# Loads of one quad put behind the inverse sums of two others, one product moved to VectorE, and the order of TensorE's products drawn anew

## Chip, cores and metric

One core of a Trainium2 chip runs the whole kernel as one program. The metric is the time of one execution on the device in microseconds, the median of several runs. The kernel takes the inputs of the reference and gives its output in float32.

## What is computed

An attention with normalised queries and keys, and behind it a pair of matrix products with h·cos(h) between them:

```python
q, k, v: (8, 12, 448, 64) float32;  tau = 0.1
q_n = q / (norm(q, axis=-1) + 1e-6);  k_n = k / (norm(k, axis=-1) + 1e-6)
scores = matmul(q_n, k_n.T) / tau
attn = exp(scores - max(scores)); attn = attn / (sum(attn) + 1e-9)
x = matmul(attn, v) with heads joined: (3584, 768)
h = x @ w_in                # (3584, 2048)
out = (h * cos(h)) @ w_out  # (3584, 768)
```

## The kernel before

**Stages.** The work goes by the 8 batches, c = 0 to 7. `m1` makes x @ w_in of a batch: 8 pairs of blocks of 128 columns, each block 6 products of TensorE (96 in all), and behind each pair ScalarE and VectorE make h·cos(h) into the tile gT (L701 and L705 on ScalarE, L703 and L707 on VectorE). `m2` makes the product with w_out: half-outputs of 16 products of 384 columns each (six or eight to a batch, by turns), each ended by a copy of PSUM into osb on VectorE (L725) and a store.

**Attention by quads.** Four heads form a quad; there are 24, three to a batch, so batch 2 needs quads 6, 7 and 8. A quad goes through these steps. `load_qk` (L402) brings Q and K through SP's DMA queue into one of three buffers each. `norm_a` squares them on GpSimd (L450) and sums the squares on VectorE (L454). `norm_b` makes the inverse norms (ScalarE L472 and L484, VectorE L487 and L490) and scales Q and K on GpSimd (L511). `turn` transposes both by DMA on SP's queue (L550). `scores` is a group of 4 products of TensorE that run side by side (L568), one group for each of the 7 parts of a quad, each followed by one exponential of 896 columns on ScalarE (L575). `av` multiplies all 7 parts with V (28 products, L585), and VectorE copies the result into AVs (L594), of which there are four.

**Inverse sums.** For quads 6 to 23 two quads share a round, as quads 8 and 9 do. `sums` makes the sums of the exponentials with 28 products (L646); `invert` takes logarithm and exponential on ScalarE (L659, L661) into the one tile Zs, spreads Zs with four DMAs to a quad into R (L667, two buffers, one for even and one for odd quads), and multiplies AVs with R into xT on GpSimd (L670). `m1` of a batch reads xT. For its first pair (or the first two) the products with the first two quads of the batch go ahead (`EARLY`), those with the third quad follow.

**The order on TensorE** is the order of the program text. While `m2` of batch c runs, the table `VISITS[c]` says how the quads of the next batches are let in: an entry (n, more) takes n items from the stream of quads, then `more` products of `m2`. `LATER` says at which part of the next quad a quad's `av` stands. The first part of a quad calls `begin`, which issues the steps that prepare the later quads: `norm_b` and `turn` of the quad two ahead, `load_qk` of the quad four ahead, `norm_a` of the quad three ahead. Score groups and `av` share three pairs of PSUM banks in turn: an item waits until the one that used its pair three items earlier has been read, by ScalarE or, for an `av`, by VectorE.

**The order on the other engines and on SP's and GpSimd's DMA queues** is made by the class `Planner` when the program is built: each operation carries a reckoned duration, each DMA a reckoned transfer time (`moves`) besides a first and a last part of 1.2 and 0.8, and the planner plays the program through and lets each engine take what is ready and due soonest. That order is then fixed; each engine waits at each instruction for what it needs. Operations with `lock=True` are not planned beside one another on VectorE and GpSimd. `lead` makes an operation due earlier.

Of the kernel before, what the change touches and what calls it, by code (L numbers as in the profile page):

```python
# [8 lines left out]
ACT = mybir.ActivationFunctionType  # L9
# [12 lines left out]
class Planner:  # L22
# [21 lines left out]
    def op(self, eng, dur, fn, r=(), w=(), after=(), dma=None, moves=0, mode="f", chain=None, keep=False, lead=0.0,  # L44
           packet=74, lock=False, key=None):
        if key is None:
            self.count += 1
            key = self.count - 1
            if self.strict:
                key += self.MOVE.get(key, 0)  # L50
            if self.count - 1 in self.FILL:
                self.idle(*self.FILL[self.count - 1], key - 0.01)
        o = Op()
        o.i, o.eng, o.dur, o.fn, o.dma, o.moves, o.mode, o.chain = (
            len(self.ops), eng, dur, fn, dma, moves, mode, chain)
        o.lat = self.FIRST + moves + self.LAST if dma else self.LAT[eng]
        o.behind, o.lead, o.packet, o.lock = None, lead, packet, lock
        o.key = key
        if keep or self.strict and eng in ("act", "dve", "pool", "sp"):
            self.tail.setdefault(eng, []).append(o)  # L60
        o.reads, o.writes = tuple(r), tuple(w)
        deps = {a.i for a in after if a is not None}
        for x in o.reads:
            if x in self.last_write:
                deps.add(self.last_write[x].i)
        for x in o.writes:
            if x in self.last_write:
                deps.add(self.last_write[x].i)
            deps.update(p.i for p in self.readers.get(x, ()))
        deps.discard(o.i)  # L70
        o.deps = sorted(deps)
        for x in o.reads:
            self.readers.setdefault(x, []).append(o)
        for x in o.writes:
            self.last_write[x] = o
            self.readers[x] = []
        self.ops.append(o)
        return o
# [200 lines left out]
def bass_cosine_attention__then__act_gcu_kernel(  # L279
# [31 lines left out]
    def ring(name, n, shape, dt):  # L311
        return [sb("%s%d" % (name, i), shape, dt) for i in range(n)]
# [20 lines left out]
    Zs = ring("Zs", 1, [128, S], F32)  # L333
    R = ring("R", 2, [128, 2, S], F32)
# [15 lines left out]
    op = P.op  # L350
# [19 lines left out]
    def table(m):  # L370
        if mode[0] == m:
            return
        mode[0] = m
        op("act", 1.3, lambda e: e.add_instruction(mybir.InstLoadActFuncSet(
            name=nc.get_next_instruction_name(), act_func_set_id={"exp": 6, "sin": 9}[m], engine=e.engine)),
           w=["table"])

    def act(m, dur, fn, r=(), w=(), **kw):
        table(m)
        return op("act", dur, fn, r=[*r, "table"], w=w, **kw)  # L380
# [16 lines left out]
    def load_one(qd, w, part=ALL[0], after=()):  # L397
        b, h0, s = qd // QB, 2 * (qd % QB), qd % 3
        src, dst, nm = ((q, Qf, "Qf"), (k, Kf, "Kf"))[w]
        j0, j1 = part  # L400
        ap = bass.AP(src.tensor, (b * NH + h0) * S * D + j0 * D, [[NJ * D, 128], [NH // 2 * S * D, 2], [1, (j1 - j0) * D]])
        return op("sp", 0.6, lambda e: e.dma_start(dst[s].ap()[:, :, j0:j1].rearrange("p r j d -> p r (j d)"), ap),  # L402
                  w=cut(nm, s, part), dma=(nm, s, j0), moves=0.17 * (j1 - j0), after=after)

    def load_qk(qd, after=()):
        return [load_one(qd, w, after=after) for w in range(2)]
# [30 lines left out]
    def square(qd, w, eng, part=ALL[0], after=()):  # L437
        s, u = qd % 3, qd % 2
        j0, j1 = part
        n = (j1 - j0) / NJ  # L440
        f, sq, nm = ((Qf, sqq, "Q"), (Kf, sqk, "K"))[w]
        src = f[s].ap()[:, :, j0:j1]
        dst = sq.ap().rearrange("p (r j) d -> p r j d", r=2)[:, :, j0:j1]
        if part == ALL[0]:
            src, dst = src.rearrange("p r j d -> p (r j) d"), sq.ap()
        if eng == "act":
            op("act", 0.1 + 0.83 * n, lambda e: e.activation(dst, src, ACT.Square), r=cut(nm + "f", s, part),
               w=cut("sq" + nm, 0, part))
        else:
            op(eng, (1.68 if eng == "pool" else 1.05) * n, lambda e: e.tensor_tensor(dst, src, src, ALU.mult),  # L450
               r=cut(nm + "f", s, part), w=cut("sq" + nm, 0, part), after=after, lock=True)

        def add():
            return op("dve", 0.07 + 0.95 * n, lambda e: e.tensor_reduce(  # L454
                out=n2.ap()[:, u, H * w:H * w + H] if part == ALL[0] else jr(n2, u, w, part),
                in_=dst, axis=AX.X, op=ALU.add),
                r=cut("sq" + nm, 0, part), w=cut("n2%d" % w, u, part))

        return add
# [55 lines left out]
    def norm_a(qd):  # L515
        for w in range(2):
            square(qd, w, "pool")()
# [28 lines left out]
    def turn(qd, after=()):  # L546

        u = qd % 3
        for n, t, nm in ((Qn, qT, "Q"), (Kn, kT, "K")):
            op("sp", 1.3, lambda e, n=n, t=t: e.dma_start_transpose(  # L550
                t[u].ap().rearrange("p j a x -> p j (a x)"), n[0].ap().rearrange("p j r d -> p (j r d)")),
               r=cut(nm + "n", 0, ALL[0]), w=cut(nm + "T", u, ALL[0]), dma=(nm + "T", u), moves=1.1, packet=18,
               after=after)
# [42 lines left out]
    Z, LEAD = 6, 15.0  # L596
# [58 lines left out]
    def invert(quads, bk):  # L655
        z = 0
        np_ = 2 * len(quads)
        zz = Zs[z].ap()[0:32 * np_, :]
        act("exp", 0.44, lambda e: e.activation(zz, bank(bk, S, 0, 32 * np_), ACT.Ln, bias=0.0, scale=1.0),  # L659
            r=whole(bk), w=[("Zs", z)], lead=LEAD)  # L660
        act("exp", 0.47, lambda e: e.activation(zz, zz, ACT.Exp, bias=0.0, scale=-1.0), r=[("Zs", z)], w=[("Zs", z)], lead=LEAD)  # L661
        for i, qd in enumerate(quads):
            u, sl, b = qd % 2, qd % NA, qd // QB
            for r in range(2):
                for a in range(2):
                    src = bass.AP(Zs[z], (64 * i + 32 * r + 16 * a) * S, [[S, 16], [0, 4], [1, S]])
                    op("sp", 0.6, lambda e, r=r, a=a, u=u, src=src: e.dma_start(R[u].ap()[64 * r:64 * r + 64, a, :], src),  # L667
                       r=[("Zs", z)], w=[("R", u, r, a)], dma=("R", u, r, a), moves=0.5, packet=140, lead=LEAD)
            c0 = 2 * (qd % QB)
            op("pool", 2.04, lambda e, u=u, sl=sl, b=b, c0=c0: e.tensor_tensor(  # L670
                xT[b % 2].ap()[:, c0:c0 + 2, :], AVs[sl].ap(), R[u].ap(), ALU.mult),
                r=[("AV", sl), *(("R", u, r, a) for r in range(2) for a in range(2))], w=[("x", b % 2, qd % QB)], lead=LEAD, lock=True)

    def round_(quads, bk):
        sums(quads, bk)
        invert(quads, bk)

    INV2PI = 1.0 / (2.0 * math.pi)
    GUARD = 1.0 - 4e-6
# [52 lines left out]
    def store(t, x0, x1, parts, engs=("sp", "sp")):  # L732
        so = t % 3
        for sg, eng in enumerate(engs):
# [8 lines left out]
    ROUNDS = [[i, i + 1] for i in range(6, NQ, 2)]  # L743
    VISITS = [
# [7 lines left out]
        [],  # L752
        [],
    ]
    LATER = {19: 3, 18: -1, 5: 3, 7: -1, 21: -2, 9: 4, 10: -2, 12: -2, 22: -1, 23: 4, 15: -2, 13: 3, 16: 1, 17: 4, 8: 1}
    E1, E2 = NNB - 6, NNB - 4
    due = []
    cur = [7]
# [1 line left out]
    def now():  # L760
        return [[o for o in P.ops if o.eng == "pe"][-1]]

    def begin(qd):
        if qd + 2 < NQ:
            norm_b(qd + 2)
            turn(qd + 2)
        if qd < NQ - 4:
            load_qk(qd + 4)
        if qd + 3 < NQ:
            norm_a(qd + 3)  # L770

    AFTER, SLOTS = 2, 3
    stream = []
# [3 lines left out]
    def quad_slots(qd):  # L777
        slots = [("s", NJ * qd + j) for j in range(NJ)]
        if qd > FIRST and qd - 1 not in closed:
            n = AFTER + LATER.get(qd, 0)  # L780
            slots[n:n] = [("z", qd - 1)] * (qd - 1 in DIRECT) + [("v", qd - 1)]
# [53 lines left out]
    gate = load_qk(1)  # L835
# [139 lines left out]
    done = FIRST  # L975
    for c in range(B):
# [59 lines left out]
        done = new  # L1036
# [46 lines left out]
```

## Time and profile before

| what | value |
|---|---|
| median of 3 runs | 422.27 us (421.94 to 424.38) |
| the profiled execution: its time | 421.43 us |
| its span, first to last instruction | 419.6 us |
| outside the span | 1.8 us |
| TensorE busy | 411.3 us, 98% |
| ScalarE busy | 308.2 us, 73% |
| VectorE busy | 268.4 us, 64% |
| GpSimd busy | 201.2 us, 48% |
| DMA | 62.84 MB, mean 150 GB/s |

The profile calls TensorE's products PE, its weight loads PEld, VectorE DVE, ScalarE ACT, GpSimd POOL, and the DMA queue of SyncE SPq. A row of the timeline has the start in us from the start of the span, the time in us, the engine, the line of the kernel, the operation, what it writes and reads, and the count; idle time of the engine and what ended it stand behind in brackets. A row of the chain has start, time, engine, tile, line. TensorE's products are pipelined, so a product counts by the distance from its start to the next one's, and the duration in a row is longer than that.

### The profile page before, as it was taken

How to read it: one execution, taken by the hardware profiler on the slowest of the kernel's cores; microseconds unless marked ns; L12 is line 12 of the kernel's file. 1: busy time of each engine (PE TensorE's matmuls, PEld its weight loads, DVE VectorE, ACT ScalarE, POOL GpSimd, SP SyncE). 2: the span in 40 equal slices, each digit the busy share in tenths (PEclk: the TensorE clock that was granted, in tenths of full speed). 3: DMA queues.
4: the chain of work that ended last, by engine and by line, in shares of the span. 5: the costliest groups of instructions: out<-in, count | busy, mean ns of one | idle time of the engine just before them, and what ended most of it. 6: DMA issues, size and time to landing. Idle time of an engine off the chain costs nothing.

```text
span 419.6 us, 8780 instructions
## 1 busy us (share of the span) xinstructions
PE 411.3 (98%) x3723; PEld 218.8 (52%) x3723; DVE 268.4 (64%) x335; ACT 308.2 (73%) x406; POOL 201.2 (48%) x137
## 2 busy tenths in 40 slices
PE   8989999999999999999999999999999999999996
PEld 8555554445545445445554555454554555555563
DVE  5876796879853769744995459724883138736931
ACT  6998789988888977788788837789788556505700
POOL 3376339792378794768538952368303303000000
PEclk9999999999999999999999999999999999999999
DMA  8999998985099979687929991399604723031032
GB/s 276 254 232 209 239 247 219 213 203 124 9 223 175 314 166 212 104 215 132 239 66 220 197 263 19 63 160 210 146 0 83 159 50 83 2 75 39 1 77 75
DMA packets 71128, 62.84 MB, mean 150 GB/s; under 512 B 40496, under 2 KB 66096, under 8 KB 71088
## 3 DMA queue, kind: packets, MB, share of 16 engines
q1 hardware_dynamic: 60688, 50.28, 50.4%
q0 software_dynamic: 10240, 11.80, 17.3%
q8 instruction: 29, 0.48, 0.5%
q10 hardware_dynamic: 160, 0.20, 0.1%
q14 instruction: 11, 0.09, 0.1%
HBM read 45.61 MB, written 11.01 MB: 135 GB/s over the span
## 4 chain that ended last, share of the span: by engine, by line
PE 88%; ACT 6%; DVE 2%; DMA 1%; POOL 1%; issue 0%; SPq 0%; ACTq 0%; POOLq 0%
PE PS L716 34%; PE PS L688 34%; PE PS L568 8%; PE PS L585 7%; ACT E L575 4%; PE PS L646 3%; PE PS L817 2%; DMA R<-Zs 1%; PE PS L607 1%; DVE osb L725 1%; POOL xT L670 0%; DVE n L454 0%; ACT ar L701 0%; ACT ar L624 0%; ACT ar L620 0%
## 5 line engine op out<-in xcount | busy, mean ns | idle before, releaser
L716 PE MATMUL PS<-W,gT 128*128 128x384 bf16 x896 | 156.6, 327 | 0.0
L575 ACT ACTIVATE E<-PS 128x896 bf16<-128x896 f32 x168 | 143.2, 917 | 17.4 <-PE PS L568 15.9
L688 PE MATMUL PS<-xT,W 128*128 128x448 bf16 x768 | 147.0, 353 | 0.7 <-POOL xT L670 0.3
L716 PEld LDWEIGHTS PS<-W,gT 128*128 128x128 bf16 x896 | 83.2, 98 | 69.2 <-issue 16.1
L688 PEld LDWEIGHTS PS<-xT,W 128*128 128x128 bf16 x768 | 74.5, 98 | 71.3 <-POOL xT L670 0.8
L701 ACT ACTIVATE ar<-PS 128x896 int32<-128x896 f32 x64 | 58.2, 911 | 42.0 <-PE PS L688 41.6
L703 DVE SCALAR_TENSOR_TENSOR ar<-ar,PS 128x896 f32<-128x896 int32 x64 | 69.1, 1084 | 24.2 <-ACT ar L701 24.2
L707 DVE TENSOR_TENSOR gT<-PS,ar 128x896 bf16<-128x896 f32 x64 | 69.4, 1088 | 7.8 <-ACT ar L705 7.4
L705 ACT ACTIVATE ar<-ar 128x896 f32<-128x896 f32 x64 | 60.5, 947 | 16.1 <-DVE ar L703 15.6
L725 DVE COPY osb<-PS 128x384 f32<-128x384 f32 x56 | 31.2, 557 | 62.0 <-PE PS L716 61.5
L670 POOL TENSOR_TENSOR xT<-AVs,R 128x896 bf16<-128x896 f32 x18 | 37.6, 2089 | 40.3 <-DMA R<-Zs 40.1
L450 POOL TENSOR_TENSOR sqq<-Qf 128x896 bf16<-128x896 f32 x22 | 36.9, 1678 | 38.6 <-DMA Qf<-in_q_dram 17.7
L511 POOL TENSOR_TENSOR Qn<-Qf,rr 128x896 bf16<-128x896 f32 x21 | 38.1, 1814 | 30.8 <-DVE rr L490 26.8
L568 PE MATMUL PS<-qT,kT 64*64 64x448 bf16 x672 | 48.5, 359 | 1.4 <-ACT E L575 1.0
L450 POOL TENSOR_TENSOR sqk<-Kf 128x896 bf16<-128x896 f32 x21 | 36.9, 1756 | 18.1 <-DVE n L454 16.2
L454 DVE TENSOR_REDUCE n<-sqq 128x14 f32<-128x896 bf16 x24 | 25.7, 1072 | 20.4 <-POOL sqq L450 16.6
L594 DVE COPY AVs<-PS 128x896 f32<-128x896 f32 x21 | 22.9, 1091 | 24.0 <-PE PS L585 24.0
L585 PE MATMUL PS<-E,Vb 64*64 64x448 bf16 x672 | 37.0, 351 | 0.1
L511 POOL TENSOR_TENSOR Kn<-Kf,rr 128x896 bf16<-128x896 f32 x18 | 30.4, 1688 | 2.1 <-DMA kT<-Kn 2.1
L568 PEld LDWEIGHTS PS<-qT,kT 64*64 64x64 bf16 x672 | 16.3, 105 | 26.6 <-issue 12.0
L454 DVE TENSOR_REDUCE n<-sqk 128x14 f32<-128x896 bf16 (+2 forms) x25 | 25.9, 1040 | 2.3 <-POOL sqk L450 2.1
L414 POOL DMA_DIRECT2D Vb<-in_v_dram x24 | 18.1, 755 | 18.1 <-PE PS L568 12.5
(49 smaller groups left out, 191.6 us busy)
## 6 DMA issues: line engine op xcount, KB each, us to landing
Qf<-in_q_dram SPq DMA_DIRECT2D x24, 448.0 KB, 4.8
out_dram<-osb SPq DMA_DIRECT2D x54, 192.0 KB, 3.2
Kf<-in_k_dram SPq DMA_DIRECT2D x23, 448.0 KB, 5.6
R<-Zs SPq DMA_DIRECT2D x72, 112.0 KB, 3.0
Vb<-in_v_dram POOLq DMA_DIRECT2D x24, 224.0 KB, 6.6
W<-in_moe_w_in_dram POOLq DMA_DIRECT2D x4, 768.0 KB, 19.6
W<-in_moe_w_out_dram POOLq DMA_DIRECT2D x4, 768.0 KB, 25.0
qT<-Qn SPq DMA_TRANSPOSE x20, 3.9
```

The source lines that it names most:

```text
L450: op(eng, (1.68 if eng == "pool" else 1.05) * n, lambda e: e.tensor_tensor(dst, src, src, ALU.mult), r=cut(nm + "f", s, part), w=cut("sq" ...
L454: return op("dve", 0.07 + 0.95 * n, lambda e: e.tensor_reduce(out=n2.ap()[:, u, H * w:H * w + H] if part == ALL[0] else jr(n2, u, w, part) ...
L511: lambda e: e.tensor_tensor(n[0].ap()[:, j0:j1].rearrange("p j r d -> p r j d"), f[s].ap()[:, :, j0:j1], rb, ALU.mult),
L568: ins = e.matmul(bank(bs + r, S, 64 * a, 64 * a + 64), kT[u].ap()[64 * r:64 * r + 64, j, a, :], qT[u].ap()[64 * r:64 * r + 64, :, a, :], s ...
L575: act("exp", 0.81, lambda e: e.activation(E[es].ap(), two(bs), ACT.Exp, bias=0.0, scale=INV_TAU), r=pair(bs), w=[("E", es)], chain="E")
L585: ins = e.matmul(bank(bk + a, S, 64 * r, 64 * r + 64), Vb[vs].ap()[64 * a:64 * a + 64, r, j, :], E[es].ap()[64 * a:64 * a + 64, r, :], sta ...
L688: ins = e.matmul(bank(bk + i2), W1.ap()[:, i, 128 * nb:128 * nb + 128], xT[c % 2].ap()[:, i, :], start=(i == 0), stop=(i == NKC - 1))
L701: op("act", 0.815, lambda e: e.activation(ar[s].ap().bitcast(I32), two(bk), ACT.Identity, bias=0.25, scale=INV2PI), r=bs, w=[("ar", s)])
L703: op("dve", 1.005, lambda e: e.scalar_tensor_tensor(ar[s].ap(), ar[s].ap().bitcast(I32), -2.0 * math.pi, two(bk), ALU.mult, ALU.add), r=bs ...
L705: act("sin", 0.86, lambda e: e.activation(ar[s].ap(), ar[s].ap(), ACT.Sin, bias=GUARD * math.pi / 2.0, scale=GUARD), r=[("ar", s)], w=[("a ...
L707: op("dve", 1.01, lambda e: e.tensor_tensor(gT.ap()[:, 2 * pr:2 * pr + 2, col:col + S], two(bk), ar[s].ap(), ALU.mult), r=bs + [("ar", s)] ...
L716: ins = e.matmul(bank(bk, HW), gT.ap()[:, f, col:col + 128], W2.ap()[:, f, HW * h:HW * h + HW], start=(f == 0), stop=(f == NNB - 1))
```

## The change

Four things are changed. (1) `invert` gives back the second of its two ScalarE operations, and `round_` passes it on: `begin` of quad 10 no longer issues `load_qk(14)` and `norm_a(13)` on the spot, but puts them off until the round whose last quad is 9 has been issued, and the load then also waits for that ScalarE operation (`gate`). (2) The product that makes x of quad 8 goes to VectorE instead of GpSimd. (3) The reckoned transfer time of the DMAs into R is 1.3 for quad 8 and 0.45 for all others, where it was 0.5. (4) `VISITS` of the batches 1 to 5 and four entries of `LATER` have other numbers.

```diff
-        act("exp", 0.47, lambda e: e.activation(zz, zz, ACT.Exp, bias=0.0, scale=-1.0), r=[("Zs", z)], w=[("Zs", z)], lead=LEAD)
+        done = act("exp", 0.47, lambda e: e.activation(zz, zz, ACT.Exp, bias=0.0, scale=-1.0), r=[("Zs", z)], w=[("Zs", z)], lead=LEAD)
...
-                       r=[("Zs", z)], w=[("R", u, r, a)], dma=("R", u, r, a), moves=0.5, packet=140, lead=LEAD)
+                       r=[("Zs", z)], w=[("R", u, r, a)], dma=("R", u, r, a), moves=1.3 if qd == 8 else 0.45, packet=140, lead=LEAD)
...
-            op("pool", 2.04, lambda e, u=u, sl=sl, b=b, c0=c0: e.tensor_tensor(
+            op(*(("dve", 1.05) if qd == 8 else ("pool", 2.04)), lambda e, u=u, sl=sl, b=b, c0=c0: e.tensor_tensor(
...
+        return done
 
     def round_(quads, bk):
         sums(quads, bk)
-        invert(quads, bk)
+        gate = invert(quads, bk)
+        if quads[-1] in BEHIND.values():
+            while put_off:
+                put_off.pop(0)([gate])
...
-        [(0, 23), (3, 5), (3, 16), (3, 13), (3, 4), (3, 11), (3, 11), (3, 8), (3, 0), (3, 0), (3, 16), (3, 8),
-         (3, 5), (3, 8), (1, 0)],
-        [(0, 19), (3, 16), (3, 15), (3, 12), (3, 9), (3, 7), (3, 6), (3, 0), (3, 0)],
-        [(0, 25), (3, 7), (3, 11), (3, 13), (3, 9), (3, 15), (3, 12), (3, 11), (3, 0)],
-        [(0, 23), (3, 12), (3, 14), (3, 16), (3, 12), (3, 5), (3, 5), (3, 0), (3, 9)],
-        [(0, 20), (3, 9), (3, 18), (3, 6), (3, 0), (3, 20), (3, 33), (3, 8), (3, 0), (1, 14)],
+        [(0, 22), (3, 6), (3, 16), (3, 13), (3, 0), (3, 16), (3, 11), (3, 8), (3, 0), (3, 0), (3, 18), (3, 8),
+         (3, 4), (3, 6), (1, 0)],
+        [(0, 20), (3, 21), (3, 17), (3, 11), (3, 8), (3, 5), (3, 4), (3, 0), (3, 0)],
+        [(0, 23), (3, 8), (3, 13), (3, 10), (3, 32), (3, 12), (3, 16), (3, 7), (3, 4)],
+        [(0, 23), (3, 12), (3, 14), (3, 12), (3, 16), (3, 5), (3, 5), (3, 0), (3, 9)],
+        [(0, 19), (3, 12), (3, 17), (3, 8), (3, 0), (3, 23), (3, 30), (3, 9), (2, 0), (2, 10)],
...
-    LATER = {19: 3, ..., 16: 1, 17: 4, 8: 1}
+    LATER = {19: 4, ..., 16: -1, 17: 1}
...
+    BEHIND = {10: 9}
+    put_off = []
+
     def begin(qd):
+        assert not put_off or BEHIND.get(qd)
         if qd + 2 < NQ:
             norm_b(qd + 2)
             turn(qd + 2)
+        steps = []
         if qd < NQ - 4:
-            load_qk(qd + 4)
+            steps.append(lambda after=(): load_qk(qd + 4, after))
         if qd + 3 < NQ:
-            norm_a(qd + 3)
+            steps.append(lambda after=(): norm_a(qd + 3))
+        if qd in BEHIND:
+            put_off.extend(steps)
+        else:
+            for f in steps:
+                f()
```

More of the change, by code (lines that the diff above doesn't have):

```diff
@@ L754, in bass_cosine_attention__then__act_gcu_kernel @@
     ]
-    LATER = {19: 3, 18: -1, 5: 3, 7: -1, 21: -2, 9: 4, 10: -2, 12: -2, 22: -1, 23: 4, 15: -2, 13: 3, 16: 1, 17: 4, 8: 1}
+    LATER = {19: 4, 18: -1, 5: 3, 7: -1, 21: -2, 9: 4, 10: -2, 12: -2, 22: -1, 23: 4, 15: -2, 13: 3, 16: -1, 17: 1}
     E1, E2 = NNB - 6, NNB - 4
```

## The prediction

> **What bounds the kernel now.** I read the page first, for which engine sets the end.
>
> ```profile
> span 419.6 us, 8780 instructions
> PE 411.3 (98%) x3723; PEld 218.8 (52%) x3723; DVE 268.4 (64%) x335; ACT 308.2 (73%) x406; POOL 201.2 (48%) x137
> PE 88%; ACT 6%; DVE 2%; DMA 1%; POOL 1%; issue 0%; SPq 0%; ACTq 0%; POOLq 0%
> ```
>
> TensorE is busy 98% of the span, and 88% of the chain that ended last is its own work. The change alters no product and no count of products, so it can give back only the time in which TensorE waits, and the time that it loses in going from one kind of product to another. Both have to be priced first, from the chain that ended last and from the waits of the weight loads after 105 us (the first stage is the same text before and after).
>
> ```profile
> 343.28 18.16 PE PS L688 x96
> 361.44 15.60 PE PS L716 x96
> 122.74 0.69 PE PS L568 x12
> 123.43 1.89 PE PS L716 x11
> PEld PS L716 <- DVE osb L725: 1.3, 4, 0.4
> PEld PS L646 <- DVE osb L725: 1.1, 2, 0.5
> PEld PS L688 <- POOL xT L670: 0.8, 1, 0.8
> ```
>
> Undisturbed, a product of L688 counts 18.16/96 = 0.189 us and one of L716 15.60/96 = 0.1625. Eleven of L716 between score groups take 1.89, not 1.79: leaving a group of another kind, or entering one, costs 0.10. Three score groups take 0.69, so one counts 0.20 and the edge again 0.10. Waits that name another engine's work come to little: twice osb around a round of sums, and once xT, at the start of `m1` of batch 2. That last one I followed in the chain and in the timelines of TensorE and of SP's queue.
>
> ```profile
> 135.74 0.58 ACT Zs L661
> ...
> 139.26 6.27 DMA R<-Zs
> 145.60 2.09 POOL xT L670
> 145.70 1.69 PE L688 MATMUL PS<-xT,W 128*128 128x448 bf16 x8
> 147.73 2.44 PE L688 MATMUL PS<-xT,W 128*128 128x448 bf16 x12 [0.35 <-POOL xT L670]
> 133.20 0.58 SPq L402 DMA_DIRECT2D Qf<-in_q_dram  x1
> 133.83 0.48 SPq L402 DMA_DIRECT2D Kf<-in_k_dram  x1
> 134.35 1.16 SPq L738 DMA_DIRECT2D out_dram<-osb  x2
> 135.56 0.59 SPq L402 DMA_DIRECT2D Qf<-in_q_dram  x1
> 136.19 1.02 SPq L402 DMA_DIRECT2D Kf<-in_k_dram  x1
> 137.31 6.25 SPq L667 DMA_DIRECT2D R<-Zs  x8
> ```
>
> Zs of quads 8 and 9 is ready at 135.74 + 0.58 = 136.32. SP is then issuing K of quad 14 and reaches the first R transfer only at 137.31. The fourth, issued at 139.26, lands at 145.53, GpSimd makes x of quad 8 until 147.69, and TensorE, whose eight products that need only quads 6 and 7 are issued by 145.70 + 8 × 0.189 = 147.21, goes on at 147.73. **The wait is 0.52 us**, the only one that the named edits aim at.
>
> **The change part by part, the load.** Behind the gate, both loads of quad 14 can be issued no earlier than the R transfers; these carry a lead of 15 and are due by `m1` of batch 2, long before quad 14's scores, so the four of quad 8 go first, at about 136.4 instead of 137.31. How much earlier they land, the DMA view of 136 to 146 tells.
>
> ```profile
> DMA  9999999999999899999999999999999999999998
> DMA packets 1988, 3.15 MB, mean 315 GB/s; under 512 B 229, under 2 KB 1838, under 8 KB 1985
> Qf<-in_q_dram SPq DMA_DIRECT2D x1, 448.0 KB, 5.7
> ```
>
> The DMA engines are loaded throughout; what stands ahead sets the landing. Taking 896 KB (0.92 MB) out from ahead at 315 GB/s gives 2.9 us: R of quad 8 lands near 142.6 (bounds: 141.5, if the issue's 0.9 comes on top; 145.5, if nothing is gained). Quad 14's loads move from 135.6 to 139 or, behind quad 9's four transfers too, to about 142; SP carries the same number of issues. The squares of quad 13 are put off with them. Quad 14's scores come at 185 (row at 185.36 below), quad 13's in the same stage, and before them lies `m1` of batch 2, 96 products or 18 us in which TensorE takes no quad. I cost this delay at nothing; without that cover it would be up to 6 us.
>
> **x of quad 8 on VectorE.** The same product with an AVs operand has stood on VectorE for quads 3 to 5 (first row: least, median, most):
>
> ```profile
> L633 DVE TENSOR_TENSOR xT<-AVs,ar x3: 1082/1092/2303, 70.5 to 85.6; 128x896 bf16<-128x896 f32 x3
> 85.57 2.30 DVE L633 TENSOR_TENSOR xT<-AVs,ar 128x896 bf16<-128x896 f32 x1
> 86.89 2.52 POOL L450 TENSOR_TENSOR sqk<-Kf 128x896 bf16<-128x896 f32 x1
> 140.75 1.49 PE L585 MATMUL PS<-E,Vb 64*64 64x448 bf16 x28
> 142.30 1.09 DVE L594 COPY AVs<-PS 128x896 f32<-128x896 f32 x1 [0.35 <-PE PS L585]
> 143.28 0.76 PE L568 MATMUL PS<-qT,kT 64*64 64x448 bf16 x12
> ```
>
> So 1.09 us, or 2.30 beside GpSimd work, against 2.09 on GpSimd. I take 1.09, the median, and keep both. From 142.6 it ends between 143.7 and 144.9; even landing at 145.53 with 1.09 gives 146.6, before 147.21. VectorE takes its instructions in order, so the question is what stands behind this one while it waits: the copy of `av` of quad 10 (142.30), which frees a pair of PSUM banks for the second of the three score groups at 143.28. By the planner's own numbers R is ready at gate + 0.15 + 0.6 + 1.2 + 4 × 1.3 + 0.8 = 136.3 + 8.0 = 144.3, the AVs copy at 142.7, so the copy is queued ahead, and x of quad 8 runs at 144 to 145.5, in time. **The wait goes: −0.52.** What is late next at this place is nothing that TensorE needs before 147.2.
>
> The Trainium skill, page "SBUF — State Buffer", section "Who interferes with whom", speaks against the move: a VectorE instruction with two SBUF inputs and a GpSimd instruction that reads SBUF exclude each other, and the later one fully waits. The pair at 85.57 and 86.89 agrees: VectorE's product took 2.30 there. By that rule the sum would hold all the same, since 144.3 + 2.30 is 146.6; what it raises is the second rival below, from 422.8 to 424.0.
>
> **The drawn order.** I wrote out both orders of TensorE's items from the tables. Up to the sums of quads 8 and 9 after has 92 products of L716 where before has 91, and one passage between kinds fewer (the sums of 6 and 7 now stand among score groups): **−0.10**. Behind these sums the fills are 18, 8, 4, 6 instead of 16, 8, 5, 8. `av` of quad 10 comes 0.06 + 0.33 = 0.39 later, its copy ends at 143.78; the score group that needs its banks comes at 143.28 + 0.21 + 0.39 − 0.16 = 143.72 and needs about 0.05 behind the copy: **+0.11**. `m1` of batch 2 starts at 145.71, as before. In the next stage the fills around `av` of quads 12 and 13 shrink by five products, two of them between quad 14's first groups and `av` of 13.
>
> ```profile
> 185.36 0.76 PE L568 MATMUL PS<-qT,kT 64*64 64x448 bf16 x12
> 188.48 0.55 PE L568 MATMUL PS<-qT,kT 64*64 64x448 bf16 x8
> 185.79 2.54 ACT L575 ACTIVATE E<-PS 128x896 bf16<-128x896 f32 x3 [0.64 <-PE PS L568]
> 188.89 1.73 ACT L575 ACTIVATE E<-PS 128x896 bf16<-128x896 f32 x2 [0.56 <-PE PS L568]
> ```
>
> The third exponential from 185.79 ends at 188.33; its banks are wanted at 188.67 (second group of the row at 188.48), 0.34 later. Those two products take 0.33 of it, and with about 0.05 for the hand-over it waits: **+0.05**. ScalarE sat idle 0.64 and 0.56 there, so its sum isn't the limit. The waits for osb stand at the same places of the order (t8.0 and sums of 10 and 11; the same pattern for 16 and 17), unchanged. In the other stages score groups and `av` are moved by at most about 1 us, once 3, against the rounds of sums that follow; those end some 20 us before the `m1` that needs them. I cost them at nothing.
>
> The reckoned transfer times add no instruction; they only shift the orders that the planner draws, and I price them with these.
>
> **Sum:** −0.52 − 0.10 + 0.11 + 0.05 = −0.46, say −0.5. On the profiled execution: 421.43 (span 419.6 and 1.8 around it) gives 420.9. The median of the runs shown is 422.27, 0.84 above this execution, and I put the forecast on it: **421.8**.
>
> **The rivals.** *First, the wait stays:* the transfers land no earlier, or VectorE comes to x of quad 8 late because norm sums are queued before it. For: DMA busy throughout. Against: 1.09 instead of 2.09 alone brings 1.0 us. It would give −0.10 + 0.16, so 422.3. *Second, slower:* x of quad 8 stands ahead of the AVs copy in VectorE's queue and holds it back; the score group at 143.72 waits for it, and TensorE behind it. The point from which it decides is x of quad 8 ending after 142.7, that is, R landing after 141.6, which my estimate of 142.6 passes; only the order in the queue saves it. Landing at 142.6 and 1.09 each, the copy ends at 144.8: 1.0 more wait. With 2.30, 2.2 more; landing at 145.53, 3.9; with both, 5.1. That is 422.8, 424.0, 425.7 or 426.9; I call it 424.0. *Third, the shorter fills:* if none of ScalarE's idle time around quads 13 and 14 covers the five products that the fills there lose (22 to 17), 5 × 0.1625 = 0.81 is lost instead of 0.05, so 422.6. *Fourth, all shown idle goes:* the two waits for osb as well. From TensorE's timeline, the first of the two:
>
> ```profile
> 170.71 1.48 PE L716 MATMUL PS<-W,gT 128*128 128x384 bf16 x7
> 172.34 1.32 PE L646 MATMUL PS<-E,sel 128*32 128x448 bf16 x24
> ```
>
> Seven products and a passage from 170.71 take 7 × 0.1625 + 0.10 = 1.24, to 171.95; the sums begin at 172.34, so 0.39 is waited. Twice that with −0.52 and −0.10 makes −1.4, so 420.9. No row speaks for it, as the order there is kept.
>
> **How the numbers follow.** Forecast 0.56 (its own range 421.2 to 422.4), first rival 0.12, second 0.17, third 0.10, fourth 0.05. A measurement of this kernel can tell from no change about 1%, or 4.2 us. Faster by that is out of reach of the idle time that the rows show: 0.01, for what they don't show. Slower by that (426.5) is the far end of the second rival, and an order drawn by reckoned times that turns out wrong at a place I priced at nothing: 0.09. Within 1%: 0.90. The range goes from 420.6, a little below the case in which all idle is gone, to 425.0, which takes in the first half of the second rival.
>
> **What would show it.** In the profile after: SP issues R of quad 8 before Q and K of quad 14, about 136.4; the landing is near 142.6; x of quad 8 is a VectorE row of 1.09 to 2.30 behind an AVs copy; the wait of L688 for xT is gone; the L568 waits grow by some 0.1 to 0.2; the osb waits stay. The prediction is wrong if VectorE shows an idle row ended by R's DMA with an AVs copy behind it, if TensorE's wait of L568 or L585 for VectorE or ScalarE grows by over 1 us, or if GpSimd stands at quad 14's load long enough to make quad 12 late at 169.

## The result: 0.3% slower

The changed kernel takes **423.65 us** (median of 22 runs, 422.17 to 426.35), the kernel before, on the same chip, 422.09 us (median of 22, 421.26 to 424.38). The ratio is 1.0032, with a 95% interval of 1.002 to 1.0044: about 1.5 us slower. That is within 1% and inside the range, but the forecast went the other way, by −0.5 us. The profiled executions differ by nearly as much: 421.43 us before, 422.85 us after.

The page of the kernel after, the rows that answer to the first fence of the prediction, and its waits of TensorE from 100 us on (engine, tile and line, what it waited for: us in total, times, the longest):

```profile
span 421.0 us, 8778 instructions
PE 411.4 (98%) x3723; PEld 218.8 (52%) x3723; DVE 270.2 (64%) x336; ACT 308.2 (73%) x406; POOL 199.9 (47%) x136
PE 83%; ACT 6%; DVE 4%; DMA 3%; POOL 1%; SPq 1%; issue 1%; POOLq 0%
```

```profile
PE PS L692 <- DVE gT L711: 1.5, 1, 1.5
PE PS L568 <- DVE AVs L594: 0.2, 1, 0.2
```

TensorE's own work has stayed, 411.4 us against 411.3, so the 1.4 us of span are idle time. TensorE's share of the chain fell from 88% to 83%, and what took its place is VectorE, DMA, GpSimd and SP's queue: a chain that runs through a load. The wait for xT is gone. A new one of 1.5 us, longer than any single wait that the prediction quotes of the kernel before, stands in `m1`: the line is L692 (L688 before), it waits for gT (L711, L707 before), and that is h·cos(h), not the attention.

**Where the named edits act, the change did what it says.** The timelines of SP's queue, VectorE, GpSimd and TensorE of the kernel after, around `m1` of batch 2:

```profile
135.46 1.86 SPq L742 DMA_DIRECT2D out_dram<-osb  x2
137.42 5.99 SPq L667 DMA_DIRECT2D R<-Zs  x8
143.45 0.67 SPq L402 DMA_DIRECT2D Qf<-in_q_dram  x1
```

```profile
141.71 1.09 DVE L454 TENSOR_REDUCE n<-sqk 128x14 f32<-128x896 bf16 x1
142.72 0.32 DVE L490 RECIPROCAL rr<-nrm 128x28 f32<-128x28 f32 x1
142.95 1.03 DVE L594 COPY AVs<-PS 128x896 f32<-128x896 f32 x1
144.19 1.59 DVE L670 TENSOR_TENSOR xT<-AVs,R 128x896 bf16<-128x896 f32 x1
```

```profile
144.77 2.55 POOL L511 TENSOR_TENSOR Kn<-Kf,rr 128x896 bf16<-128x896 f32 x1
```

```profile
144.03 0.57 PE L568 MATMUL PS<-qT,kT 64*64 64x448 bf16 x8 [0.18 <-DVE AVs L594]
...
145.93 4.33 PE L692 MATMUL PS<-xT,W 128*128 128x448 bf16 x22
```

The fourth of the R transfers, the last of quad 8, starts the row of a view from 140 us on; below it stand the times from issue to landing of the third and the fourth (least, median, most):

```profile
139.48 3.93 SPq L667 DMA_DIRECT2D R<-Zs  x5
...
DMA to landing us min/median/max: 3.4/3.6/3.8
```

SP issues R at 137.42 and quad 14's load only behind it, at 143.45. That is no earlier than before (137.31), but the fourth transfer now lands 3.4 us after its issue, at 142.9, where it took 6.27 us and landed at 145.53. x of quad 8 stands on VectorE behind the AVs copy and ends at 144.19 + 1.59 = 145.78, before `m1` starts at 145.93, and the 22 products there run on without a gap.

**The new wait is 110 us later, in `m1` of batch 4.** The timelines of VectorE and TensorE of the kernel before, and then of the kernel after:

```profile
246.34 1.09 DVE L454 TENSOR_REDUCE n<-sqq 128x14 f32<-128x896 bf16 x1 [2.25 <-POOL sqq L450]
247.34 1.08 DVE L703 SCALAR_TENSOR_TENSOR ar<-ar,PS 128x896 f32<-128x896 int32 x1
...
252.53 2.09 DVE L707 TENSOR_TENSOR gT<-PS,ar 128x896 bf16<-128x896 f32 x2
...
243.32 18.34 PE L688 MATMUL PS<-xT,W 128*128 128x448 bf16 x96
```

```profile
245.30 1.09 DVE L454 TENSOR_REDUCE n<-sqk 128x14 f32<-128x896 bf16 x1 [4.29 <-POOL sqk L450]
247.73 1.09 DVE L454 TENSOR_REDUCE n<-sqq 128x14 f32<-128x896 bf16 x1 [0.88 <-POOL sqq L450]
248.73 1.08 DVE L707 SCALAR_TENSOR_TENSOR ar<-ar,PS 128x896 f32<-128x896 int32 x1
...
253.92 2.09 DVE L711 TENSOR_TENSOR gT<-PS,ar 128x896 bf16<-128x896 f32 x2
...
243.07 11.51 PE L692 MATMUL PS<-xT,W 128*128 128x448 bf16 x60
256.07 6.98 PE L692 MATMUL PS<-xT,W 128*128 128x448 bf16 x36 [1.49 <-DVE gT L711]
```

After 60 products TensorE needs the banks that the third gT frees. Before, that gT ended at 252.53 + 2.09 = 254.62, and TensorE was there at 243.32 + 60 × 0.189 = 254.66: it had 0.04 us to spare, which the hand-over alone takes (0.06 after, from 256.01 to 256.07), and nothing in the list of waits shows such a place. After, TensorE is there at 243.07 + 60 × 0.189 = 254.41, the third gT ends at 256.01, and it goes on at 256.07: 1.66 us lost. Of the 1.4 us by which gT is late, all is there at VectorE's first step of `m1`, 248.73 instead of 247.34. That step has no idle time in front of it. In front of it stands the norm sum of a later quad, at 247.73, which waited for its square on GpSimd. The chain says what the square waited for, SP's queue why that was late, and GpSimd's timeline what stood ahead of the square (all of the kernel after, then SP's queue and GpSimd before):

```profile
240.48 5.47 DMA Qf<-in_q_dram
...
246.02 1.69 POOL sqq L450
```

```profile
237.03 2.13 SPq L550 DMA_TRANSPOSE qT<-Qn  x1
...
240.48 0.60 SPq L402 DMA_DIRECT2D Qf<-in_q_dram  x1
```

```profile
235.26 1.69 POOL L511 TENSOR_TENSOR Qn<-Qf,rr 128x896 bf16<-128x896 f32 x1 [2.17 <-DMA qT<-Qn]
237.85 4.13 POOL L670 TENSOR_TENSOR xT<-AVs,R 128x896 bf16<-128x896 f32 x2 [0.90 <-DMA R<-Zs]
...
243.57 1.69 POOL L450 TENSOR_TENSOR sqk<-Kf 128x896 bf16<-128x896 f32 x1
```

```profile
239.39 1.34 SPq L402 DMA_DIRECT2D Qf<-in_q_dram  x1
...
241.29 1.26 SPq L550 DMA_TRANSPOSE qT<-Qn  x1
...
235.50 1.68 POOL L450 TENSOR_TENSOR sqk<-Kf 128x896 bf16<-128x896 f32 x1
```

Q of quad 21 is issued 1.1 us later than before (240.48, 239.39), lands at 245.95, is squared until 247.71, and its sum holds VectorE until the first step of h·cos(h) can run. A load that TensorE doesn't need for tens of microseconds holds TensorE, because its sum is queued, on an engine that works in order, ahead of work that TensorE needs at once. In SP's queue stands why the load is late: the transpose of Q of quad 19 (237.03, for 2.13 us) now goes ahead of it, where before it came behind (241.29).

The load is only half of it. GpSimd works in a fixed order too, and the K square of quad 20, done from 235.50 on before, now stands behind the scaling of Q of quad 19, which waits 2.17 us for a transpose, and behind two products x. It ends at 243.57 + 1.69 = 245.26. Even with Q of quad 21 there in time, its square could have started at 245.27 at the earliest; it started at 246.02, and at 244.62 before. So of the 1.4 us about 0.75 are the load's and 0.65 GpSimd's order's.

The gains and losses of the profiled executions, counted by the distance between starts on TensorE beyond an undisturbed one: −0.51 (xT), −0.10 (one passage fewer), +0.37 (the score groups behind the AVs copy), +1.66 (gT of batch 4), and +0.04 to +0.07 at several small places. That is about +1.5, against +1.4 in the span.

### The profile page after: what moved, and what is told of

Its sections match the earlier page's. It is cut to its first block, busy times and chain, and to the rows that moved or that the text cites. A ratio compares the mean times of both kernels' runs of the same rounds, so it can differ in the third digit from the quotient of the medians.

```text
span 421.0 us, 8778 instructions
## 1 busy us (share of the span) xinstructions
PE 411.4 (98%) x3723; PEld 218.8 (52%) x3723; DVE 270.2 (64%) x336; ACT 308.2 (73%) x406; POOL 199.9 (47%) x136
## 4 chain that ended last, share of the span: by engine, by line
PE 83%; ACT 6%; DVE 4%; DMA 3%; POOL 1%; SPq 1%; issue 1%; POOLq 0%
PE PS L720 32%; PE PS L692 31%; PE PS L568 7%; PE PS L585 6%; ACT E L575 4%; PE PS L646 3%; DMA Qf<-in_q_dram 2%; PE PS L831 2%; PE PS L607 1%; DVE n L454 1%; DVE ar L707 1%; POOL sqq L450 1%; DVE gT L711 1%; DMA R<-Zs 1%; DVE osb L729 1%
## 5 line engine op out<-in xcount | busy, mean ns | idle before, releaser
L692 PE MATMUL PS<-xT,W 128*128 128x448 bf16 x768 | 147.0, 353 | 1.8 <-DVE gT L711 1.5
L692 PEld LDWEIGHTS PS<-xT,W 128*128 128x128 bf16 x768 | 74.6, 98 | 72.4 <-DVE gT L711 1.9
L707 DVE SCALAR_TENSOR_TENSOR ar<-ar,PS 128x896 f32<-128x896 int32 x64 | 69.0, 1083 | 21.0 <-ACT ar L705 21.0
L711 DVE TENSOR_TENSOR gT<-PS,ar 128x896 bf16<-128x896 f32 x64 | 69.4, 1088 | 7.8 <-ACT ar L709 7.4
L670 POOL TENSOR_TENSOR xT<-AVs,R 128x896 bf16<-128x896 f32 x17 | 35.5, 2092 | 39.9 <-DMA R<-Zs 39.9
L568 PE MATMUL PS<-qT,kT 64*64 64x448 bf16 x672 | 48.7, 359 | 1.5 <-ACT E L575 1.0
L585 PE MATMUL PS<-E,Vb 64*64 64x448 bf16 x672 | 37.1, 350 | 0.1
L511 POOL TENSOR_TENSOR Kn<-Kf,rr 128x896 bf16<-128x896 f32 x18 | 31.3, 1737 | 0.0
L568 PEld LDWEIGHTS PS<-qT,kT 64*64 64x64 bf16 x672 | 16.4, 105 | 27.1 <-issue 10.9
```

The costliest lines, as they stand in the source:

```text
L511: lambda e: e.tensor_tensor(n[0].ap()[:, j0:j1].rearrange("p j r d -> p r j d"), f[s].ap()[:, :, j0:j1], rb, ALU.mult),
L568: ins = e.matmul(bank(bs + r, S, 64 * a, 64 * a + 64), kT[u].ap()[64 * r:64 * r + 64, j, a, :], qT[u].ap()[64 * r:64 * r + 64, :, a, :], s ...
L585: ins = e.matmul(bank(bk + a, S, 64 * r, 64 * r + 64), Vb[vs].ap()[64 * a:64 * a + 64, r, j, :], E[es].ap()[64 * a:64 * a + 64, r, :], sta ...
L692: ins = e.matmul(bank(bk + i2), W1.ap()[:, i, 128 * nb:128 * nb + 128], xT[c % 2].ap()[:, i, :], start=(i == 0), stop=(i == NKC - 1))
L707: op("dve", 1.005, lambda e: e.scalar_tensor_tensor(ar[s].ap(), ar[s].ap().bitcast(I32), -2.0 * math.pi, two(bk), ALU.mult, ALU.add), r=bs ...
L711: op("dve", 1.01, lambda e: e.tensor_tensor(gT.ap()[:, 2 * pr:2 * pr + 2, col:col + S], two(bk), ar[s].ap(), ALU.mult), r=bs + [("ar", s)] ...
```

## The experiments

My theory was that the new tables of products, above all that of batch 3, had moved SP's work so that quad 21's load and with it the norm sums came late. The rival was that the named edits (gate, VectorE, reckoned times) did that by themselves. Ratios are to executions of the kernel before taken alongside, with 95% intervals. The first two expectations call the load issued at 240.48 and the sums behind it quad 20's; they are **quad 21's**, and the late K sum at 245.30 is quad 20's. The squares of all quads go through one tile for Q and one for K, so what moves quad 20's sums moves quad 21's too.

**Table of batch 3 as before.** The kernel after with

```diff
-         [(0, 23), (3, 8), (3, 13), (3, 10), (3, 32), (3, 12), (3, 16), (3, 7), (3, 4)],
+         [(0, 25), (3, 7), (3, 11), (3, 13), (3, 9), (3, 15), (3, 12), (3, 11), (3, 0)],
-    LATER = {..., 16: -1, 17: 1}
+    LATER = {..., 16: 1, 17: 4}
```

> The changed kernel with VISITS of batch 3 and the entries 16 and 17 of LATER as they were before; all else as changed. Queue theory (SP issues the load of quad 20 about 1 us later under the new table of batch 3, VectorE stands in order at the norm sums of quad 20 ahead of the first steps of m1 of batch 4, TensorE runs out of PSUM banks there): the wait for gT of 1.5 to 1.65 us falls to 0 to 0.3, time about 422.0, ratio to before 0.997 to 1.001. Rival (the new place of x of quad 8 and the gate push work downstream, whatever the table of batch 3): the wait stays over 1 us, time about 423.6.

Measured: 422.66 us, ratio 0.9998 (0.9978 to 1.0018). Its waits of TensorE:

```profile
PE PS L692 <- DVE gT L711: 0.8, 1, 0.8
PE PS L568 <- DVE AVs L594: 0.8, 1, 0.8
```

The interval lies just below that of the kernel after (1.002 to 1.0044), so this table carries part of the loss, by a narrow margin. But the wait for gT, which was to shrink to 0.3 or less, is half as long and stays, at the same 61st product, and in this one execution the AVs copy took back what it gave. The theory in this narrow form missed: the table of batch 3 is not the sole cause.

**Norm sums of quad 20 behind the second pair of `m1` of batch 4.** The kernel after, in which `square` can be told to wait and `norm_a` keeps the two sums of quad 20 until that pair has been issued:

```diff
+    LATE = {20: (4, 1)}
+    behind_m1 = {}
...
-            square(qd, w, "pool")()
+            add = square(qd, w, "pool")
+            if qd in LATE:
+                behind_m1.setdefault(LATE[qd], []).append(add)
+            else:
+                add()
...  (behind the pair pr of m1 of batch c)
+            for add in behind_m1.pop((c, pr), ()):
+                add(after=[P.ops[-1]])
```

> The changed kernel, but the two norm sums of quad 20 on VectorE wait for the second pair of m1 of batch 4, so that they can't stand ahead of its first steps; tables, gate and x of quad 8 as changed. Queue theory: the wait for gT goes to 0, VectorE's first step of that m1 starts near 246.5 instead of 248.7, time 423.65 - 1.6 = about 422.0. Rival (m1 of batch 4 is too tight for VectorE in any order, since it starts 0.25 us earlier): over 1 us of wait stays, time over 423.2.

Measured: **421.66 us, ratio 0.9976 (0.9955 to 0.9998)**: faster than after, and a little faster than before (the interval ends just under 1). SP's load of Q of quad 21, then VectorE and TensorE in `m1` of batch 4:

```profile
242.39 0.60 SPq L402 DMA_DIRECT2D Qf<-in_q_dram  x1
...
246.66 1.09 DVE L714 SCALAR_TENSOR_TENSOR ar<-ar,PS 128x896 f32<-128x896 int32 x1 [2.66 <-ACT ar L712]
252.20 2.19 DVE L718 TENSOR_TENSOR gT<-PS,ar 128x896 bf16<-128x896 f32 x2
...
243.24 18.32 PE L699 MATMUL PS<-xT,W 128*128 128x448 bf16 x96
```

The first step now waits for ScalarE alone and starts at 246.66, the third gT ends at 254.39 at the latest, and the 96 products run through. SP issues Q of quad 21 still later in this run, at 242.39, and TensorE doesn't notice. That shows it: the wait was made by the sums' place in VectorE's queue, and the late load only filled it.

**The named edits with the old tables,** that is the kernel before with gate, VectorE and reckoned times.

> Before with the gate, x of quad 8 on VectorE and the new reckoned transfer times, but the old tables. Queue theory: no wait for gT over 0.3 us, the wait for xT of 0.5 gone, 0 to 0.4 new wait for the AVs copy of quad 10: 421.6 to 422.0, ratio 0.998 to 1.000. Rival (these parts cause the loss): 423.2 or more.

Measured: 424.33 us, ratio 1.0036 (1.0019 to 1.0052). TensorE's waits, and SP's queue in the same kernel and then in the kernel before:

```profile
PE PS L568 <- DMA kT<-Kn: 1.4, 1, 1.4
PE PS L692 <- DVE gT L711: 0.9, 1, 0.9
```

```profile
175.29 5.09 SPq L667 DMA_DIRECT2D R<-Zs  x8
180.43 1.39 SPq L550 DMA_TRANSPOSE qT<-Qn  x1
181.86 1.65 SPq L550 DMA_TRANSPOSE kT<-Kn  x1
```

```profile
174.31 1.29 SPq L550 DMA_TRANSPOSE qT<-Qn  x1
...
177.23 5.16 SPq L667 DMA_DIRECT2D R<-Zs  x8
```

The wait for xT is gone here as well, but the edits are slower without the new tables too. Quad 14's load is put off from 135.56 to 142.93. Its transposes come behind the eight R transfers, six microseconds later than before (180.43, 174.31), and its second score group waits 1.4 us for kT. That the put-off load is what places them there isn't shown: with the new tables alone, the load not put off, they stand behind the R transfers too (185.47 behind 180.32). The 0.9 for gT in batch 4 is there as well. By its mark (423.2 or more) the rival came out, and the queue theory's limit of 0.3 for gT did not hold; but the next run shows that the tables cost as well. Each set of edits moves SP's order, and each alone makes the wait for gT.

**The new tables alone,** in the kernel before.

> Before with the new tables alone. Queue theory: the wait for xT of about 0.5 stays, and a wait for gT near 1.6 at batch 4 appears: about 423.7 to 424.2, ratio 1.004 to 1.005. Rival (the parts cause the loss): no wait for gT over 0.3, about 422.1.

Measured: 426.87 us, ratio 1.0098 (1.006 to 1.0135). Waits, and SP's queue:

```profile
PE PS L688 <- POOL xT L670: 2.9, 1, 2.9
PE PS L688 <- DVE gT L707: 2.4, 2, 1.7
```

```profile
138.39 0.72 SPq L402 DMA_DIRECT2D Qf<-in_q_dram  x1
139.97 6.70 SPq L667 DMA_DIRECT2D R<-Zs  x8
```

With these tables and without the gate, SP issues quad 14's load ahead of R at 138.39, and R at 139.97 instead of 137.42: the wait for xT grows to 2.9 us. Both gT waits stand in batch 4. The time is above what either theory gave; the profiled execution is the slowest of six, 429.46 us, and TensorE's own work is 2.2 us longer in it too (413.5, against 411.3). What the edits cost doesn't add up: +0.36% for the parts, +0.98% for the tables, +0.32% for both.

**Which sum it is.** In four kernels `LATE` named quad 21 instead of 20. Those sums come to the list only when it has been emptied, so all four **leave out the two norm sums of quad 21**, 2.2 us of VectorE's time. First the kernel after so changed:

> The changed kernel with only the two norm sums of quad 21 put behind the second pair of m1 of batch 4 (the sums that stand ahead of that m1 are quad 21's; the run before moved quad 20's, and with them 21's). Queue theory: these two alone make the wait for gT; it goes to 0, the K sum of quad 20 still ahead of them ends in time; ratio to before 0.997 to 0.999. Rival (the late K sum of quad 20 holds VectorE just as well): a wait for gT over 0.5 stays, ratio over 1.000.

Measured: 422.2 us, ratio 0.9991 (0.9963 to 1.0019). Waits and VectorE:

```profile
PE PS L699 <- DVE gT L718: 0.8, 1, 0.8
...
246.54 1.09 DVE L454 TENSOR_REDUCE n<-sqk 128x14 f32<-128x896 bf16 x1 [5.54 <-POOL sqk L450]
```

Half of the wait stays even when quad 21's sums aren't there: quad 20's K sum comes after 5.54 us in which VectorE stood waiting for GpSimd. Both quads' sums hold VectorE, each because it waits in its turn for a square that GpSimd makes late; that fits the shares worked out above. Then the kernel before so changed:

> The kernel before with the norm sums of quad 21 put behind in the same way and nothing else. Queue theory: before waits there for nothing (third gT 0.05 us ahead of TensorE), so the ratio is 0.999 to 1.001 in an undisturbed execution, and at most 0.002 lower if its executions over 422.5 are those in which this place waits. Rival (putting the sums behind is what makes the second run faster, wherever it is done): ratio 0.9976 as there.

Measured: 422.57 us, ratio 1.0003 (0.9972 to 1.0035): taking the sums away brings nothing where they don't hold TensorE. Its profiled execution, 425.92 us, shows something else, in the waits and SP's queue:

```profile
PE PS L695 <- POOL xT L677: 3.7, 1, 3.7
...
139.68 5.79 SPq L674 DMA_DIRECT2D R<-Zs  x8
```

SP's queue has the same order there as in the kernel before, which waits 0.3 for xT by the same list of TensorE's waits (0.8 in that of the weight loads), with R at 137.31. Here R goes at 139.68. SP is behind earlier in this execution: by 1.2 us at the R transfers ahead of these (126.06, against 124.89), and the transpose behind them then takes 2.23 us to issue instead of 1.28. So one profiled execution doesn't give the size of that wait. Next, the kernel after without quad 21's sums and **without the gate** (`BEHIND = {}`):

> As the first of this call, but without the gate: loads of quad 14 issued as soon as their buffer is free. Theory that the gate brings R of quad 8 forward: R is issued from 137.3 to 140 and lands after 145.5, x of quad 8 ends after 147.2, a wait for xT of 0.5 to 2 us; ratio 1.001 to 1.004. Rival (VectorE alone does it, the gate is idle): no wait for xT, ratio as the first of this call.

Measured: 423.88 us, ratio 1.0022 (0.9993 to 1.0052); it waits 2.3 us for xT. And with **x of quad 8 on GpSimd** again (the gate kept):

> As the first of this call, but x of quad 8 on GpSimd as before. Theory that the gate alone is enough: R lands near 143, GpSimd's 2.09 us end by 146, no wait for xT; ratio 0.996 to 0.999, the wait for the AVs copy unchanged at 0.4. Rival (the move to VectorE is needed, since GpSimd is at other work): a wait for xT over 0.5, ratio over 1.000.

Measured: 422.25 us, ratio 0.9987 (0.9961 to 1.0014); no wait for xT, 0.3 for gT and 0.5 for the AVs copy. This points to the gate as what removes the wait, not VectorE.

**The parts once more, with nothing left out.** Now each as one edit to the kernel with quad 20's sums put off. Without the gate:

```diff
-    BEHIND = {10: 9}
+    BEHIND = {}
```

> The changed kernel with the norm sums of quad 20 behind the second pair of m1 of batch 4 (as in the second run, nothing left out) and without the gate. Theory that the gate brings R of quad 8 forward: a wait for xT of 1 to 3 us comes back, ratio 1.001 to 1.006. Rival (the gate is idle, the sums alone make the second run fast): ratio 0.997 to 0.999, no wait for xT over 0.3.

Measured: 424.11 us, ratio 1.0047 (1.002 to 1.0075). Waits and VectorE:

```profile
PE PS L699 <- DVE xT L677: 1.5, 1, 1.5
...
146.89 2.27 DVE L677 TENSOR_TENSOR xT<-AVs,R 128x896 bf16<-128x896 f32 x1
```

With these tables **the gate is worth about 0.7%** (1.0047 against 0.9976, the intervals apart, each against its own executions of the kernel before). R is issued from 137.46 on, nearly as with the gate (137.09), but its fourth transfer lands 7.4 us after its issue, at 146.9, instead of 3.9: what the gate takes away is the load that stands ahead in the DMA engines. VectorE alone doesn't save the wait, since R lands late and the product then takes 2.27. Putting off quad 20's sums in the kernel **before**:

> The kernel before with the norm sums of quad 20 behind the second pair of m1 of batch 4, and nothing else. Theory: at that place before waits for nothing in its profiled execution, its loss is the wait for xT, which stays at 0.5 us or more: ratio 0.998 to 1.001. Rival (the sums alone are the gain of the second run): ratio 0.9976 or lower.

Measured: 422.9 us, ratio 1.0008 (0.9989 to 1.0026), with the waits for xT (1.4) and the AVs copy (0.8) as they come there. So the step that helped after brings nothing before. Together with the run without the gate this points to the gate as the source of the gain over the kernel before; the gate with the old tables and quad 20's sums put off was not run. With x of quad 8 on **GpSimd**:

```diff
-            op(*(("dve", 1.05) if qd == 8 else ("pool", 2.04)), lambda ...
+            op("pool", 2.04, lambda ...
```

> The second run with x of quad 8 on GpSimd as before. Theory that the gate is enough: no wait for xT over 0.2 us, ratio 0.996 to 0.999, like the second run. Rival (VectorE is needed): a wait for xT over 0.5 us, ratio over 1.000.

Measured: 421.77 us, ratio 0.9986 (0.9975 to 0.9998), no wait for xT. The interval overlaps that of the kernel with VectorE: moving the product isn't needed. Last, that kernel with the two fills ahead of `m1` of batch 2 as **6, 4 instead of 4, 6**:

> The run before with the fills around av of quad 10 as 6 and 4 products instead of 4 and 6, so that the score group that needs the AVs copy comes 0.33 us later. Theory of the bank wait: that wait of 0.4 to 0.7 falls by 0.3, the first products of m1 move by nothing; ratio 0.0005 to 0.001 lower than the run before, too little to tell by time, to be read in the waits. Rival (VectorE, not the distance, sets it): the wait stays.

Measured: 421.78 us, ratio 0.9988 (0.9976 to 1.0001). The wait for the AVs copy goes, and one of 0.4 for ScalarE's exponentials (L582) takes its place ahead of `m1`. No gain.

## Why the prediction was wrong

- **The step that failed** is the one about the other stages: groups "are moved by at most about 1 us, once 3, against the rounds of sums that follow; those end some 20 us before the `m1` that needs them. I cost them at nothing." No wait for xT arose from the rounds, but of the some 20 us little was left at batch 4 once R and x are counted: the products x of quads 14 and 15 ran from 237.85 to 241.98, and `m1` started at 243.07. And I asked only what TensorE's moved items need themselves. What moved with them was the preparation that `begin` issues, through SP and GpSimd to sums on VectorE, whose queue `m1` shares. `m1` of batch 4 had 0.04 us to spare; a norm sum 1.4 us later made 1.66 there. That one term, with the AVs copy below, turns −0.5 into +1.4. The prediction did name an order that turns out wrong at a place priced at nothing, but only as a way to lose over 4.2 us. The reckoned times "I price with these": also at nothing, and not tested alone.
- **The wait for xT** went, −0.51 against −0.52 in these executions, and by the way that was named. One link was off: SP was to reach R at 136.4; it did so at 137.42. The two stores ahead of R were there before too (134.35, 1.16 us); now they came at 135.46 and took 1.86, as SP was 1.1 us later already at the load of quad 13 (134.30, against 133.20). The gain in issue time was nothing. The gain in landing was the 2.9 us of the sum: the fourth transfer took 3.4 us instead of 6.27 and landed at 142.9, where I had 142.6. The size of the wait was one execution's: in kernels with the same order in SP's queue there it was 3.7 and 1.4 (the runs with sums left out of, or put off in, the kernel before).
- **VectorE's order** was as worked out: the AVs copy at 142.95 ahead of x of quad 8, 1.59 us for the latter, inside 1.09 to 2.30. The second rival did not come about.
- **The AVs copy** was sized at +0.11 and cost 0.37. Its mechanism holds. A norm sum and a reciprocal stood ahead of it (141.71, 142.72), so it ended at 143.98, not 143.78: the same mistake as in batch 4, on a small scale.
- **Quad 14's scores** (+0.05) showed a wait of 0.06 (188.58 to 189.12 for the two groups, against 188.48 to 188.96), and the waits for osb stayed, both as forecast. The third rival did not come about.
- **The delay of quad 14's load at nothing** holds after, but not as a matter of course: after, too, quad 14's transposes come behind eight R transfers (179.99, against 174.31 before), and in the run with the old tables the second of them made a wait of 1.4 us. The 18 us without score groups that I named as cover were not all of the way; SP's queue with eight R transfers lies on it too.
- **The test of wrongness** that I wrote watched L568 and L585, and GpSimd at quad 14's load. The wait came at L692, which it did not watch.
- **A row passed over:** the list of the weight loads' waits also names ScalarE's exponentials, 2.5 us ahead of score groups and 1.4 ahead of `av`. I left them out without a reason. TensorE's own list from 100 us on, which names xT alone (0.3), shows that they cost nothing there.

Left open: how much of the late load of quad 21 comes from the table of batch 3 and how much from the others (the run with that table of before shows half the wait, in one execution), and what first puts SP behind in the executions in which it issues R over 2 us later with one order.

## What to carry to other kernels

Where an engine works in order and serves both a critical stage and preparation for later, look up what stands directly ahead of the critical instruction there, and what that waits for: a place with no wait in the profile can have 0.04 us to spare, and the list of waits doesn't show it. Compute the slack at each such place before costing a reordering at nothing, and move preparation that depends on a load behind the critical steps, as the 421.66 us version does. An edit that shields one transfer can be right and still come out slow; test it with the new wait taken away (here 1.0032 became 0.9976) before it is dropped.

## What the runs showed of the hardware that I had not expected

- The product of VectorE with two SBUF inputs, 1.09 us by itself in the prediction's rows, took 1.59 in the kernel after and 2.27 without the gate. Each time a product of GpSimd was under way when it started: in the kernel after one of 1.70 from 143.12 on, without the gate one of 1.68 from 146.52 on. VectorE's ended 0.96 us behind that one's end (145.78 behind 144.82, 149.16 behind 148.20), nearly its time by itself, and GpSimd's next product was longer in its turn (2.55 and 2.52). The Trainium skill, page "SBUF — State Buffer", section "Who interferes with whom", says that such a pair excludes each other; the trace agrees, and the one that comes later waits. The prediction's row at 85.57 fits in the same way, but it named the wrong partner: VectorE's 2.30 there come from the GpSimd product at 85.25, and the one at 86.89 waited for VectorE.
- With one order in its queue, SP issued the R transfers of quad 8 at 137.31 in one execution and at 139.68 in another; TensorE's wait for xT was 0.3 and 3.7 us by the same list. A single profiled execution gives such a term's sign, not its size.
